# The projection stage's planner: reciprocal deviations gated on GpSimd, low parts kept off VectorE, and two turns of tokens in one slot

## The chip, the core and the metric

The kernel runs on one core of a Trainium2 chip. The metric is the device time of one execution in microseconds; lower is better. Engines are named as the profile names them: PE is TensorE (PEld is its weight load, which overlaps PE), DVE is VectorE, ACT is ScalarE, POOL is GpSimd, SP is SyncE. Every engine works through its own queue in the order in which the program wrote it, and waits where an operand is not there yet.

## What is computed

One transformer block on 2048 tokens of 640 features, in float32: a normalisation, attention with 32 heads of 20 features, a residual sum, a second normalisation, and a gated feed-forward part with 1728 inner features.

```python
def _layernorm(x, axis=-1, eps=1e-5):
    m = jnp.mean(x, axis=axis, keepdims=True)
    v = jnp.var(x, axis=axis, keepdims=True)
    return (x - m) / jnp.sqrt(v + eps)

qkv = x @ wqkv                       # x normalised: 2048x640 @ 640x1920
scores = jnp.einsum("bhqd,bhkd->bhqk", q, k) * (Dh ** -0.5)
o = jnp.einsum("bhqk,bhkd->bhqd", softmax(scores), v)
h = x + o @ wo
h2 = h + (silu(z @ w_gate) * (z @ w_up)) @ w_down    # z: h normalised
```

## The kernel before, in words

The tokens go in four chunks of 512, and each chunk in four tiles of 128. The kernel has three stages: the **projections** (q, k and v of all chunks), attention, and the feed-forward part. The change touches the projections alone, which fill roughly the first 324 us.

**Products in float32 precision.** Each operand is split into a high part (ScalarE, L97) and a low part, which is the operand less its high part (L98, on the engine that `split` is given). A product is three matmuls: high by high, high by low, low by high. `query_key` makes a block of 128 columns of q or k for a chunk (15 matmuls of 512 columns), `value` a tile of v (15 matmuls of 320 columns). All these are L573 in the profile. The array is used as two halves of 64 rows, and each of the 15 matmuls comes twice, once for each half, so that a block is 30 rows of the trace.

**The work list.** `work` is a list of 72 slots: blocks of chunk 0, then for each chunk its 10 blocks mixed with the 8 value tiles of the chunk before, then the last value tiles. Chunk c's first block stands in slot `begins(c) + 2` (slots 12, 30 and 48). In slots `begins(c) - 3` to `begins(c) + 1` the chunk's normalised tokens are turned (transposed), feature tile by feature tile, five in all, one to a slot.

**A turn** (`flip`, L787) is 16 small transposes on PE (L793) into two PSUM banks, two copies to SBUF and the high part on ScalarE (L801 twice, then L97 into `z_hi`), and the low part `z_lo` on VectorE or GpSimd (L98). `before_flip` asks the planner for two free banks first. Blocks and value tiles of the chunk need `z_hi` of all five turns at once, as their first five matmuls, and `z_lo` in their last five.

**Normalisation of a chunk** (`norm`, L759) is a list of 14 items, `lns`, handed out two to a slot: four of statistics (L133, L134 on VectorE), six that hold the eleven steps of the reciprocal deviation on 128x4 elements (`rstd_steps`: a first guess by integer arithmetic and three Newton steps, L107 on VectorE), and four that apply it (L765, on GpSimd for chunks 2 and 3). Turns start when `lns` is empty.

**Filling products.** Attention needs, for each query, the largest score ahead of the exponentials. Part of these score products is made in this stage, between the projection's matmuls, from finished blocks that were stored to DRAM and loaded again ("staged", `load_items`). GpSimd forms the difference of two staged key tiles in place (L433). Each pair of products is one or two matmuls (L195, L218), a rectification on ScalarE (L206, L232) and a sum with maximum on VectorE (L208 and L225, each with a short read of the maximum). VectorE's instruction frees the PSUM bank. There are eight banks; projections, turns and filling products share them.

**The planner.** `Halves` (L534) writes all this as one order. It keeps its own clock of each half of PE and of VectorE, ScalarE, GpSimd, SyncE and the DMAs, in `free`, with a fixed duration for each operation (for instance 1.3 us for a low part on GpSimd and 0.75 us on VectorE, L532), and issues whatever its clocks say is ready. So a change of one rule alters the order of PE, ScalarE, VectorE and GpSimd from there to the stage's end, though not what is computed. Which engine makes a low part is chosen in `second_part` (L661). It is called by `flip` for `z_lo` and by `keep` (L843), which stores a finished block: PSUM to SBUF (L352), high part (L97) and low part (L98) into a buffer that the trace calls `e`, `q_stk` or `v_stk`, whichever lent place is used.

Of the kernel before, what the change touches and what calls it, by code (L numbers as in the profile page):

```python
# [50 lines left out]
def tile_block(ctx: ExitStack, tc: tile.TileContext, x, wqkv, wo, wg, wu, wd, out):  # L51
# [287 lines left out]
    with tc.tile_pool(name="pa", bufs=2) as pa:  # L339
# [186 lines left out]
        def next_pair():  # L526
# [2 lines left out]
            queues = (others, early) if first else (early, others)  # L529
            return next((queue for queue in queues if queue and queue[0][0]()), None)  # L530

        SECOND = (("pool", 1.3), ("vector", 0.75))  # L532

        class Halves:  # L534
# [125 lines left out]

            def second_part(self, after):  # L661
                ends = [max(self.free[e], after, self.now()) + us for e, us in SECOND]
                if ends[1] + 1.0 < ends[0] and self.free["vector"] < after + 0.5:
                    return nc.vector, self.use("vector", SECOND[1][1], after)
                return nc.gpsimd, self.use("pool", SECOND[0][1], after)

# [92 lines left out]
        def norm(c):  # L759

            mv = pa.tile([P, TPC, 2], F32, name="mv")
            r, steps = rstd_steps(pa, mv[:, :, 1], TPC, "a")

            def apply(t):
                (nc.gpsimd if c > 1 else nc.vector).tensor_scalar(  # L765
                    xs[c * TPC + t], xs[c * TPC + t], mv[:, t, 0:1], r[:, t : t + 1],
                    op0=ALU.subtract, op1=ALU.mult,
                )

            return (  # L770
                [
                    (("vector", 1.1), lambda t=t: stats(pa, xs[c * TPC + t], mv[:, t, :]), c)
                    for t in range(TPC)
                ]
                + [(("vector", 0.35), lambda f=f, g=g: (f(), g()), c) for f, g in zip(steps[::2], steps[1::2] + [lambda: None])]
                + [
                    (("pool", 2.55) if c > 1 else ("vector", 0.75), lambda t=t: apply(t), c)
                    for t in range(TPC)
                ]
            )  # L780
# [161 lines left out]
        for at, (kind, c, *which) in enumerate(work):  # L942
# [70 lines left out]
                load_values(0, 0, NT - TPC)  # L1013
            last = any(at == begins(n) + 1 for n in range(1, NC))
            for _ in range(99 if last else 4 if 4 <= at < 7 else 2):
                if at >= 2 and lns and (pe.now() >= x_at[lns[0][2]] or last):
                    normed = pe.use(*lns[0][0], normed) + 0.2
                    lns.pop(0)[1]()
            for _ in range(99 if last else 1):
                if flips and not lns and (pe.now() >= normed or last):  # L1020
                    flip(*flips.pop(0))
            if at == len(work) - 6:
# [1078 lines left out]
```

## Time and profile before

| | us |
|---|---|
| median of 3 runs | 2024.7 |
| the 3 runs | 2026.38, 2024.70, 2023.99 |
| the profiled execution's own time | 2026.52 |
| its span, first to last instruction | 2024.7 |
| PE busy, of that span | 2002.5 |
| VectorE busy | 1620.2 |
| ScalarE busy | 1460.2 |
| GpSimd busy | 779.8 |
| granted PE clock (1 is full speed) | 1.00 |

All stretches of the trace are given from the span's start. A row of the timeline has the start, the duration (of all merged instructions), the engine, line and operation, what is written and read, the shapes, a count, and in brackets the idle time of the engine before it with what ended that. A row of the waits has who waited for whom, the total, how often, and the longest. A row of the groups has the count, then the busy time and the mean duration of one in ns, then idle time before. A PE matmul's end is modelled, so the start of the next weight load (PEld) shows a stop of PE better than the busy time does.

### The profile page before, as it was taken

What the parts mean: (1) busy time and instruction counts of PE and PEld (TensorE: products, weight loads), DVE (VectorE), ACT (ScalarE), POOL (GpSimd) and SP (SyncE); (2) the same over time, 40 slices, a digit from 0 to 9 for tenths busy, and PEclk for the clock granted to TensorE, in tenths of its full rate; (3) what the DMA queues carried; (4) which work ended last, traced back from release to release, by engine and by line L of the source; (5) the groups of instructions that cost most, each with busy time, mean ns of one, the idle gap of its engine ahead of it and who ended that gap; (6) DMA issues with size and microseconds to landing.
All of it is one profiled execution on the core that took longest, in us unless ns stands there. A gap on an engine that the chain in (4) does not pass through costs nothing.

```text
span 2024.7 us, 39120 instructions
## 1 busy us (share of the span) xinstructions
PE 2002.5 (99%) x13714; PEld 1237.8 (61%) x13714; DVE 1620.2 (80%) x3257; ACT 1460.2 (72%) x2944; POOL 779.8 (39%) x1075
## 2 busy tenths in 40 slices
PE   8999999999999999999999999999999999999998
PEld 7898896333333333333333333345598888888888
DVE  8869678888888888888888888886378666676667
ACT  4888888999999999999999999986633222212221
POOL 4454451243524334344520011011146444764555
PEclk9999999999999999999999999999999999999999
DMA  7866663433443534435333122221159654974542
GB/s 234 257 198 192 190 191 108 135 116 117 140 128 106 161 117 142 145 123 166 123 134 102 33 71 73 81 62 49 46 185 323 206 189 154 352 272 159 204 148 93
DMA packets 205205, 304.91 MB, mean 151 GB/s; under 512 B 47648, under 2 KB 82720, under 8 KB 203984
## 3 DMA queue, kind: packets, MB, share of 16 engines
q1 hardware_dynamic: 204768, 302.24, 45.7%
q8 instruction: 109, 1.79, 0.4%
q14 instruction: 88, 0.72, 0.1%
q10 hardware_dynamic: 240, 0.17, 0.0%
HBM read 205.78 MB, written 95.68 MB: 149 GB/s over the span
## 4 chain that ended last, share of the span: by engine, by line
PE 95%; DVE 2%; ACT 1%; issue 1%; POOL 1%; DMA 0%; SPq 0%; ACTq 0%; DVEq 0%; POOLq 0%
PE banks L1394 25%; PE banks L1384 17%; PE banks L1562 17%; PE banks L239 12%; PE banks L573 9%; PE banks L1656 8%; PE banks L1113 3%; PE banks L218 3%; PE banks L195 1%; PE banks L836 0%; PE banks L264 0%; DVE st L133 0%; DMA o_t<-o_d 0%; PE banks L1145 0%; PE banks L793 0%
## 5 line engine op out<-in xcount | busy, mean ns | idle before, releaser
L1390 ACT ACTIVATE probs<-banks 128x512 f32<-128x512 f32 x2048 | 1056.2, 612 | 58.1 <-PE banks L1384 25.9
L245 DVE TENSOR_REDUCE mx<-banks 128x1 f32<-128x512 f32 x1472 | 925.1, 684 | 116.3 <-PE banks L239 62.6
L1384 PE MATMUL banks<-q_stk,k_stk 62*128 62x512 f32 x2048 | 581.3, 429 | 1.1 <-ACT probs L1390 1.1
L1394 PE MATMUL banks<-probs,v_stk 128*32 128x512 f32 x4096 | 544.3, 604 | 0.0
L239 PE MATMUL banks<-k_stk,q_stk 60*128 60x512 f32 x1472 | 486.5, 438 | 0.2
L1384 PEld LDWEIGHTS banks<-q_stk,k_stk 62*128 62x128 f32 x2048 | 290.4, 185 | 284.4 <-ACT probs L1390 270.3
L239 PEld LDWEIGHTS banks<-k_stk,q_stk 60*128 60x128 f32 x1472 | 244.2, 184 | 162.5 <-DVE mx L245 127.1
L1780 DVE TENSOR_TENSOR tmp<-banks,tmp 128x512 f32<-128x512 f32 x208 | 141.1, 689 | 114.5 <-PE banks L1562 89.0
L1394 PEld LDWEIGHTS banks<-probs,v_stk 128*32 128x32 f32 x4096 | 80.9, 108 | 182.0 <-issue 170.1
L1656 PE MATMUL banks<-halves,yp 128*128 128x320 f32 x1032 | 178.7, 308 | 0.2 <-DVE h L1661 0.2
L1656 PEld LDWEIGHTS banks<-halves,yp 128*128 128x128 f32 x1032 | 165.1, 188 | 16.0 <-DVE h L1661 0.5
L1562 PE MATMUL banks<-t,units 128*128 128x512 f32 x624 | 162.7, 396 | 0.1
L98 POOL TENSOR_TENSOR yp<-y,yp 128x256 fp32r<-128x256 f32 x96 | 60.5, 630 | 190.4 <-ACT yp L97 176.2
L1562 PE MATMUL banks<-z,units 128*128 128x512 f32 x516 | 133.7, 394 | 0.0
L256 POOL CAST both<-neg 128x16 fp32r<-128x16 f32 x32 | 6.6, 208 | 312.0 <-PE banks L239 187.1
L1562 PEld LDWEIGHTS banks<-t,units 128*128 128x128 f32 x624 | 112.5, 188 | 18.9 <-DVE tmp L1780 0.4
L1661 DVE TENSOR_TENSOR h<-banks,h 128x320 f32<-128x320 f32 x248 | 109.9, 480 | 8.6 <-POOL h L1694 4.3
L225 DVE CUSTOM_DVE_ANT_0 q_stk<-banks,q_stk 128x512 f32<-128x512 f32 x140 | 92.5, 687 | 24.1 <-PE banks L218 14.5
L573 PE MATMUL banks<-z_hi,w_hi 64*128 64x512 f32 x380 | 105.6, 396 | 2.3 <-ACT z_hi L97 2.0
L573 PE MATMUL banks<-z_lo,w_hi 64*128 64x512 f32 x380 | 105.2, 393 | 0.0
L1562 PEld LDWEIGHTS banks<-z,units 128*128 128x128 f32 x516 | 93.2, 187 | 15.9
L573 PE MATMUL banks<-z_hi,w_lo 64*128 64x512 f32 x380 | 101.8, 391 | 0.0
(218 smaller groups left out, 2900.8 us busy)
## 6 DMA issues: line engine op xcount, KB each, us to landing
units<-w_d SPq DMA_DIRECT2D x186, 256.0 KB
w_d<-stage SPq DMA_DIRECT2D x106, 256.0 KB
halves<-j_d SPq DMA_DIRECT2D x70, 320.0 KB
k_stk<-qk_d SPq DMA_DIRECT2D x112, 160.0 KB
j_d<-stage SPq DMA_DIRECT2D x42, 320.0 KB
q_stk<-qk_d SPq DMA_DIRECT2D x64, 160.0 KB
k_stk<-qk_d SPq DMA_DIRECT2D x112, 80.0 KB
rb<-r_d SPq DMA_DIRECT2D x32, 256.0 KB
```

What stands on the lines that cost most here:

```text
L218: nc.tensor.matmul(ps, q[rows, pair, t * P : (t + 1) * P], k[rows, pair, :], start=True, stop=True)
L225: nc.vector.tensor_tensor_reduce(out=place, in0=ps, in1=place, scale=1.0, scalar=LEAST, op0=ALU.add, op1=ALU.max, accum_out=mx[:, b, pair, ...
L239: nc.tensor.matmul(ps, queries[u][rows, pair, t * P : (t + 1) * P], keys[u // NC][rows, pair, kc * CH : (kc + 1) * CH], start=True, stop=True,
L245: nc.vector.tensor_reduce(mxs[u][:, b, pair, t, kc : kc + 1], ps, axis=AX.X, op=ALU.max)
L573: product = nc.tensor.matmul(job["ps"][:, :out], lhs, rhs, start=(half == 0 and i == 0), stop=(half == 1 and i == job["n"] - 1),)
L1384: nc.tensor.matmul(ps, keys[u // NC][rows, p, kt * P : (kt + 1) * P], queries[u][rows, p, :], start=True, stop=True,)
L1390: nc.scalar.activation(probs[p][:, b, :], ps, AF.Exp, scale=scale)
L1394: nc.tensor.matmul(acc[32 * j : 32 * j + 32, :], values[u // NC][:, kt, j * VW : j * VW + 32], probs[j // 2][:, j % 2, :], start=(kt == 0) ...
L1562: nc.tensor.matmul(ps.rearrange("p (t n) -> p t n", t=TPC), w[k][:, i], z[k][:, :, j], start=(first and m == 0), stop=(last and m == len(n ...
L1656: nc.tensor.matmul(ps, a, b, start=(n == 0), stop=(n == len(pairs) - 1))
L1661: nc.vector.tensor_tensor(out=h, in0=ps, in1=h, op=ALU.add)
L1780: add = lambda out, ps, x: nc.vector.tensor_tensor(out=out, in0=ps, in1=x, op=ALU.add)
```

## The change

Three rules of the planner are altered.

```diff
+        NEWTON = "vector", 0.35
         SECOND = (("pool", 1.3), ("vector", 0.75))
...
             def second_part(self, after):
                 ends = [max(self.free[e], after, self.now()) + us for e, us in SECOND]
+                ends[1] = max(ends[1], self.free["pool"] + SECOND[1][1])
                 if ends[1] + 1.0 < ends[0] and self.free["vector"] < after + 0.5:
                     return nc.vector, self.use("vector", SECOND[1][1], after)
                 return nc.gpsimd, self.use("pool", SECOND[0][1], after)
...
-                + [(("vector", 0.35), lambda f=f, g=g: (f(), g()), c) for f, g in zip(steps[::2], steps[1::2] + [lambda: None])]
+                + [(NEWTON, lambda f=f, g=g: (f(), g()), c) for f, g in zip(steps[::2], steps[1::2] + [lambda: None])]
...
             for _ in range(99 if last else 4 if 4 <= at < 7 else 2):
-                if at >= 2 and lns and (pe.now() >= x_at[lns[0][2]] or last):
+                alone = not lns or lns[0][0] != NEWTON or pe.free["pool"] <= pe.now()
+                if at >= 2 and lns and (pe.now() >= x_at[lns[0][2]] and alone or last):
                     normed = pe.use(*lns[0][0], normed) + 0.2
                     lns.pop(0)[1]()
-            for _ in range(99 if last else 1):
+            for _ in range(99 if last else 1 + any(at == begins(n) for n in range(1, NC))):
                 if flips and not lns and (pe.now() >= normed or last):
                     flip(*flips.pop(0))
```

- An item of the reciprocal deviation is handed out only in a slot at which the planner's clock of GpSimd has run out, or in the slot `begins(c) + 1`, in which everything left is handed out.
- VectorE's end of a low part is reckoned from GpSimd's clock too. Since VectorE is taken only when its end is more than 1.0 us ahead of GpSimd's, and the two ends now differ by 1.3 - 0.75 = 0.55 us at most, VectorE is not taken at all: the seven low parts that it had in this stage after slot 8 are all GpSimd's.
- In slot `begins(c)` two turns may be made instead of one.

Counted over the whole program, PE, ScalarE and SyncE keep their numbers of instructions; VectorE has seven fewer, and GpSimd seven more.

On VectorE, in chunk 2's turns (the end of `begins(2) - 2` and of `begins(2) - 1`), the difference of the two orders reads as follows. L225 is the sum with maximum of a filling product, which frees a bank, and its second row the read of the maximum.

```order
 L225 ISA v_stk_117,mx_126<-banks,v_stk_117 128x512
 L225 ISA mx_126 128x1
-L98 TENSOR_TENSOR z_lo<-xt,z_hi 128x512
 L225 ISA q_stk,mx_126<-banks,q_stk 128x512
 L225 ISA mx_126 128x1
 L225 ISA q_stk,mx_126<-banks,q_stk 128x512
 L225 ISA mx_126 128x1
-L98 TENSOR_TENSOR v_stk_117<-v_stk_117 128x512
 L225 ISA v_stk_117,mx_126<-banks,v_stk_117 128x512
 L225 ISA mx_126 128x1
```

Both low parts have left VectorE's queue; nothing stands in their place.

On PE, the last turn of chunk 2 and what follows it. In the order of before, `z_hi_583` belongs to chunk 1 and `z_hi_1790` to chunk 2; 512 columns are a block, 320 a value tile.

```order
L573 MATMUL banks_100<-z_lo_584,w_hi_163 128x512
L573 MATMUL banks_100<-w_hi_163,z_hi_583 128x320
L793 MATMUL banks_100<-ident_101,xt_895 128x64 x8
L218 MATMUL banks_100<-k_stk0_116,raw_672 128x512
L573 MATMUL banks_100<-w_hi_163,z_hi_583 128x320
L573 MATMUL banks_100<-z_hi_1790,w_hi_163 128x512
L573 MATMUL banks_100<-w_hi_163,z_hi_583 128x320 x2
L573 MATMUL banks_100<-z_hi_1790,w_hi_163 128x512
```

In the order of the change, lines are one to three higher, and the chunks' parts are `z_hi_583` and `z_hi_1776`.

```order
L574 MATMUL banks_100<-z_hi_583,w_hi_163 128x512 x2
L795 MATMUL banks_100<-ident_101,xt_884 128x64 x8
L574 MATMUL banks_100<-z_hi_583,w_hi_163 128x512
L795 MATMUL banks_100<-ident_101,xt_884 128x64 x8
L574 MATMUL banks_100<-w_hi_163,z_hi_583 128x320 x2
L574 MATMUL banks_100<-z_hi_583,w_lo_164 128x512
L574 MATMUL banks_100<-w_hi_163,z_hi_583 128x320 x2
L574 MATMUL banks_100<-z_hi_583,w_lo_164 128x512
L218 MATMUL banks_100<-raw_674,raw_672 128x512
```

Two turns now follow each other, one slot earlier; the first matmul that reads `z_hi_1776` stands 26 rows (32 matmuls) after the last transposes, where before it was the third row after them.

On PE, the last turns of chunk 3 in the order of the change. Here the reciprocal deviations of the chunk come later, so that the turns begin two slots later (at `begins(3) - 1`), and the last two are in the last slot; `z_hi_2907` is chunk 3's.

```order
L574 MATMUL banks_100<-z_lo_1777,w_hi_163 128x512
L795 MATMUL banks_100<-ident_101,xt_2047 128x64 x8
L574 MATMUL banks_100<-w_hi_163,z_hi_1776 128x320 x2
L795 MATMUL banks_100<-ident_101,xt_2047 128x64 x8
L574 MATMUL banks_100<-z_hi_2907,w_hi_163 128x512
L574 MATMUL banks_100<-w_hi_163,z_hi_1776 128x320
L574 MATMUL banks_100<-z_hi_2907,w_hi_163 128x512
L574 MATMUL banks_100<-w_hi_163,z_hi_1776 128x320 x2
```

Before, one turn stood there instead of two, and it too was followed at once by the chunk's first block.

## Prediction, made before the run

> **What bounds the kernel now.** I read the page's chain first, then the busy times by stretch. The chain of the whole execution is PE:
>
> ```profile
> ## 4 chain that ended last, share of the span: by engine, by line
> PE 95%; DVE 2%; ACT 1%; issue 1%; POOL 1%; DMA 0%; SPq 0%; ACTq 0%; DVEq 0%; POOLq 0%
> ```
>
> The reader is to see that nothing but a shorter PE order, or fewer stops of PE, can shorten the kernel. The columns below are PE, PEld, DVE, ACT and POOL busy. The first row is the projection stage, the next two are stretches of it, the last is attention:
>
> ```profile
> 20.00:324.00 304.00, 298.10 (x2811) 276.32 (x2810) 238.33 (x833) 241.36 (x530) 139.94 (x117) 1.00 0.67 207
> 120.00:150.00 30.00, 27.90 (x276) 25.88 (x274) 19.75 (x55) 25.96 (x53) 14.40 (x11) 1.00 0.62 193
> 150.00:180.00 30.00, 28.46 (x276) 26.45 (x275) 28.68 (x87) 22.94 (x42) 13.63 (x9) 1.00 0.66 211
> 340.00:360.00 20.00, 20.00 (x144) 7.71 (x136) 17.93 (x30) 19.46 (x40) 0.42 (x2) 1.00 0.01 2
> ```
>
> Attention has PE busy in all its 20 us, so it hides nothing that the stage ahead of it loses: a microsecond saved in the projections starts attention a microsecond earlier, and I carry it to the end of the kernel in full. In the projections PE stops for little, the clock is 1.00, and GpSimd is idle for over half of the time. So the next view is who PE's weight loads wait for in that stage:
>
> ```profile
> PEld banks L218 <- DVE mx L225: 3.0, 6, 2.0
> PEld banks L573 <- ACT z_hi L97: 2.6, 2, 1.4
> PEld banks L793 <- DVE mx L208: 1.9, 4, 1.2
> PEld banks L573 <- DVE mx L225: 1.3, 1, 1.3
> PEld banks L195 <- DVE mx L208: 0.4, 1, 0.4
> PEld banks L264 <- POOL e L98: 0.4, 1, 0.4
> ```
>
> That is 6.6 us for VectorE (3.0 + 1.9 + 1.3 + 0.4) and 2.6 us for the high part of a turn, most of it in five single waits. They are what the change can win. GpSimd itself is waited for once, 0.4 us.
>
> **Part 1: low parts leave VectorE.** What each of them costs now:
>
> ```profile
> L98 DVE TENSOR_TENSOR v_stk<-v_stk 128x512 fp32r<-128x512 f32 x2 | 3.6, 1794 | 0.0
> L98 DVE TENSOR_TENSOR e<-e 128x512 fp32r<-128x512 f32 x3 | 3.3, 1094 | 6.0 <-ACT e L97 6.0
> L98 DVE TENSOR_TENSOR z_lo<-xt,z_hi 128x512 fp32r<-128x512 f32 x1 | 1.2, 1160 | 1.4 <-ACT z_hi L97 1.4
> L98 DVE TENSOR_TENSOR q_stk<-q_stk 128x512 fp32r<-128x512 f32 x1 | 0.7, 691 | 0.6 <-ACT q_stk L97 0.6
> L98 POOL TENSOR_TENSOR e<-e 128x512 fp32r<-128x512 f32 x15 | 19.5, 1297 | 53.3 <-ACT e L97 45.1 <-DMA xt<-qk_d 5.0 <-DMA raw<-qk_d 3.2
> ```
>
> Seven instructions, 3.6 + 3.3 + 1.2 + 0.7 = 8.8 us of VectorE, though alone one takes 0.69 us. On GpSimd the seven take 7 x 1.30 = 9.1 us of the 164 us (304 - 139.94) in which it is idle. Two of the big waits of PE stand right behind such an instruction. VectorE, GpSimd and PE at 52 us and at 130 us:
>
> ```profile
> 51.94 1.78 DVE L98 TENSOR_TENSOR v_stk<-v_stk 128x512 fp32r<-128x512 f32 x1
> 51.43 1.75 POOL L433 TENSOR_TENSOR k_stk<-k_stk 128x512 fp32r<-128x512 f32 x1
> 54.11 0.13 PEld L793 LDWEIGHTS banks<-ident,xt 64*128 64x128 f32 x1 [1.17 <-DVE mx L208]
> ...
> 127.55 1.16 DVE L98 TENSOR_TENSOR z_lo<-xt,z_hi 128x512 fp32r<-128x512 f32 x1 [1.43 <-ACT z_hi L97]
> 129.85 1.81 DVE L98 TENSOR_TENSOR v_stk<-v_stk 128x512 fp32r<-128x512 f32 x1
> 125.60 5.51 POOL L433 TENSOR_TENSOR k_stk<-k_stk,raw 128x512 fp32r<-128x512 f32 x4
> 132.32 0.18 PEld L573 LDWEIGHTS banks<-w_hi,z_hi 64*128 64x128 f32 x1 [1.33 <-DVE mx L225]
> ```
>
> VectorE's 0.69 us instruction takes 1.8 us while GpSimd works, the sums with maximum behind it free their banks late, and PE stops for 1.17 and 1.33 us. With those instructions gone from VectorE's queue the sums start at once. I count both waits as won: **-2.5 us**, between 0 (if the next sum is late for another reason; ScalarE, which feeds it, is busy 25.96 of 30 us there) and -6.6 (all waits for VectorE go). What is late next: the stored blocks. On GpSimd they take 0.6 us longer and queue. Nothing of PE reads them directly; they go by a DMA to filling products some slots later. I cost that at nothing, with the filling products that are ready meanwhile as cover.
>
> **Part 2: reciprocal deviations.** The third big wait is theirs, in chunk 3:
>
> ```profile
> 159.40 1.24 DVE L107 TENSOR_SCALAR v_a<-mv 128x4 f32<-128x4 f32 x1
> 160.67 1.22 DVE L107 TENSOR_SCALAR r_a<-v_a 128x4 int32<-128x4 int32 x1
> 161.93 1.19 DVE L107 SCALAR_TENSOR_TENSOR t_a<-r_a,v_a 128x4 f32<-128x4 f32 x1
> 163.15 0.16 DVE L107 TENSOR_TENSOR t_a<-t_a,r_a 128x4 f32<-128x4 f32 x1
> 159.31 2.56 POOL L433 TENSOR_TENSOR raw<-raw,k_stk 128x512 fp32r<-128x512 f32 x2 [4.34 <-DMA raw<-qk_d]
> 161.82 1.28 POOL L98 TENSOR_TENSOR v_stk<-v_stk 128x512 fp32r<-128x512 f32 x1
> 163.97 0.18 PEld L218 LDWEIGHTS banks<-raw,q_stk 60*128 60x128 f32 x1 [1.96 <-DVE mx L225]
> ```
>
> Three GpSimd instructions of 1.28 us, and three steps that end with them and take 1.2 us where the fourth takes 0.16: 3.65 instead of about 0.5 us, in the stretch where VectorE is busy 28.68 of 30 us. PE stops for 1.96 us. But the new rule is no guard against this very case. It asks the planner's clock of GpSimd, and the instruction that was in the way had waited 4.34 us for a DMA: the trace's GpSimd runs later than a fixed duration says. What helps is that the steps now stand elsewhere, 14 sums later, and only in slots for which the planner has nothing left on GpSimd. The other stretched step is in chunk 2:
>
> ```profile
> 83.08 0.79 DVE L107 TENSOR_SCALAR v_a<-mv 128x4 f32<-128x4 f32 x1
> ```
>
> It takes 0.6 us over the 0.16 of an undisturbed one and PE did not stop behind it. I take the 1.96 us as won and put one such stretch of 0.6 us back on the path: **-1.4 us**, between -1.96 (no step is met) and +1.2 (three are met again, all on the path: 3 x 1.05 = 3.2 less 1.96).
>
> On this the Trainium skill speaks against the gate as it is built. SBUF — State Buffer, "Who interferes with whom", says that a VectorE instruction with two SBUF inputs, or one in a two-port mode, and a GpSimd instruction that reads SBUF exclude each other, and that whichever issues first holds up the other. The rows above agree (0.16 us against 1.2). By that rule only what GpSimd really does when a step issues counts, so the gate is worth its 1.96 us only if the real idle time meets the planner's; by the planner's own view it would be worth 1.96 in full, and my -1.4 lies between.
>
> **Part 3: two turns in one slot.** The last turn of chunks 2 and 3 makes PE wait for its high part. ScalarE and PE, first at 140 us, then PE at 225 us:
>
> ```profile
> 139.34 0.61 ACT L352 ACTIVATE e<-banks 128x512 f32<-128x512 f32 x1
> 139.98 0.63 ACT L97 ACTIVATE e<-e 128x512 fp32r<-128x512 f32 x1
> 140.51 0.64 ACT L801 ACTIVATE xt<-banks 128x256 f32<-128x256 f32 x2
> 141.19 0.63 ACT L97 ACTIVATE z_hi<-xt 128x512 fp32r<-128x512 f32 x1
> 141.87 0.18 PEld L573 LDWEIGHTS banks<-z_hi,w_hi 64*128 64x128 f32 x1 [1.18 <-ACT z_hi L97]
> ...
> 225.47 0.18 PEld L573 LDWEIGHTS banks<-z_hi,w_hi 64*128 64x128 f32 x1 [1.40 <-ACT z_hi L97]
> ```
>
> A finished block (0.64 + 0.53 us, from start to start) and the turn (0.68 + 0.63) stand in line on ScalarE. In chunk 2 the change puts 32 matmuls between the last turn and the first use. By the stretch from 120 to 150 us (276 matmuls in 30 us, 0.109 us each) they take 3.5 us against 2.6 us for two turns on ScalarE (2 x 1.31): covered, **-1.2 us**. In chunk 3 the last two turns are both in the last slot, and the block follows at once. ScalarE has one more turn to do there, 1.3 us, but PE has it to make too and no sum of a filling product comes between, so I let that wait stand: 0, between -1.4 and +1.3. Chunk 1 has no such wait to win.
>
> **The order as a whole.** From chunk 1's third turn on all four orders differ, with the same number of matmuls, so PE streams as long as before. New waits of banks are to be expected where old ones were; no row can show them. The nearest rows are the five waits themselves, 1.17 to 1.96 us. I put back one of 1.4 us, between 0 and 5.6 (all four that I counted as won return: 1.17 + 1.33 + 1.96 + 1.18).
>
> **Sum.** -2.5 - 1.4 - 1.2 + 1.4 = -3.7 us. The profiled execution took 2026.5 us with a span of 2024.7, so it would take 2022.8 with a span of 2021.0. It lies 1.8 us over the median of the runs, 2024.7; the forecast for the median is 2024.7 - 3.7 = 2021.0.
>
> **Rivals.**
>
> *The waits move, and nothing is won.* VectorE is busy 28.68 of 30 us from 150 to 180; a queue that full makes PE wait somewhere whichever instruction is taken out. For it: ScalarE is at 25.96 of 30 where two of the waits stand. Against it: the waits are few and single, each behind one long instruction. All four return, and the time is 2024.7, give or take 1.5.
>
> *VectorE's relief reaches further.* All 6.6 us of waits for VectorE go, and chunk 2's 1.2: -7.8, 2016.9. For it: VectorE loses 8.8 us of low parts and up to 3.8 us of stretched steps. Against it: 1.0 us of these 6.6 are many waits of some 0.2 to 0.4 us, which look like the rhythm of the order.
>
> *GpSimd becomes the engine that is waited for.* The seven parts stand ahead of staged differences (L433) and of `z_lo` in its one queue. It decides from the point where its lateness, 9.1 us more of work and its waits for DMAs, exceeds what the planner leaves between a part and its use on PE:
>
> ```profile
> POOL k_stk L433 <- DMA k_stk<-qk_d: 15.1, 3, 8.2
> ```
>
> A part queued behind the longest of these is 8.2 us late. At most PE sees all 9.1 us: 9.1 - 3.7 = +5.4, 2030.1. Against it: GpSimd is idle for 54% of the stage, and PE now waits for it 0.4 us in all. A page of the Trainium skill stands on this side: GPSIMD Engine Reference, "4.1 Engine selection", puts elementwise work on VectorE and calls GpSimd about twice as slow for two inputs. The trace agrees on the ratio (1.297 against 0.691 us); by that rule alone the seven parts would cost 7 x 0.6 = 4.2 us.
>
> *The gate does nothing of what it says*: it is part of the first rival, as the steps would be met by GpSimd as before and only other waits go.
>
> **How the numbers follow.** Forecast, 0.55, with a range of its own from -6 to -1.5 (2018.7 to 2023.2). Waits move, 0.22. Relief reaches further, 0.15. GpSimd is waited for, 0.08. A measurement of this kernel can tell about 0.2%, 4.05 us, from no change, so faster means under 2020.65. Somewhat under half of the forecast's chance lies there (0.25), and all of the second rival's (0.15): 0.40. Slower by over 0.2%: 0.08. The rest, 0.52, is within 0.2%. The range goes from the second rival's 2016.9, less 0.9 for the scatter of the runs, 2016.0, to the first's upper end and as much scatter, 2027.0; GpSimd's case is left out.
>
> **What would show it.** Part 1: no L98 on VectorE's timeline from 50 to 324 us but those that read a bank, and no PEld wait over 1 us for L208 or L225 during the turns of chunks 1 and 2. Part 2: L107's largest durations under 0.8 us, at most one over 1. Part 3: the wait of L573 for `z_hi` once instead of twice, in chunk 3. The stage should end (last L573) 3 to 4 us earlier, and attention take as long as before. I am wrong if waits for POOL appear on PE, if a new wait over 1.5 us stands at another place, or if the stage ends earlier and the kernel does not.

## The result, and the profile after

| | before | after |
|---|---|---|
| median of 20 runs each | 2028.45 us | 2022.93 us |
| lowest and highest | 2023.99 to 2033.09 | 2019.93 to 2027.77 |
| ratio, 95% interval | | 0.9977 (0.9971 to 0.9983) |
| the profiled execution's own time | 2026.52 | 2023.31 |
| its span | 2024.7 | 2021.5 |
| last projection product starts at | 323.81 | 320.31 |
| from there to the end | 1700.92 | 1701.18 |

The kernel became 0.23% faster: 4.7 us by the ratio, 5.5 us by the medians, 3.2 us by the two profiled spans. In these two profiled executions the whole difference lies in the projections, whose end came 3.5 us earlier; the rest took as long as before. The windows of the changed kernel (columns as before) show the same three stretches:

```profile
20.00:324.00 304.00, 301.25 (x2822) 281.35 (x2825) 228.27 (x829) 243.58 (x538) 150.37 (x125) 0.99 0.67 209
120.00:150.00 30.00, 30.00 (x302) 28.96 (x299) 22.70 (x72) 27.94 (x57) 16.65 (x14) 1.00 0.71 216
150.00:180.00 30.00, 30.00 (x291) 28.16 (x289) 27.40 (x96) 26.56 (x51) 8.94 (x7) 1.00 0.66 205
340.00:360.00 20.00, 20.00 (x145) 7.90 (x146) 17.95 (x30) 19.58 (x40) 0.42 (x2) 1.00 0.01 2
```

By the modelled ends, PE has no stop left from 120 to 180 us. VectorE has 10 us less to do in the stage and GpSimd 10 us more. One figure of the first row is new: the granted clock is 0.99, not 1.00. The waits of PE's weight loads in the stage:

```profile
PEld banks L574 <- ACT z_hi L97: 2.1, 2, 1.4
PEld banks L218 <- ACT q_stk L232: 0.9, 4, 0.3
PEld banks L195 <- DVE mx L208: 0.7, 1, 0.7
PEld banks L795 <- DVE xt L767: 0.5, 1, 0.5
PEld banks L218 <- DVE mx L225: 0.4, 2, 0.2
```

Waits for VectorE fell from 6.6 us to 1.7 (these three rows and a smaller one of 0.2), and none is over 0.7. PE does not wait for GpSimd. Summed over all releasers (idle times of the weight loads over 0.15 us, from 20 us to the last projection product), the waits are 6.05 us, against 12.13 before. So 6.1 us of waits went, but the stage won only 3.5. The difference lies at the first row, chunk 3's `z_hi`. ScalarE's row of turns there, and the two weight loads that wait for it:

```profile
211.51 0.60 ACT L352 ACTIVATE e<-banks 128x512 f32<-128x512 f32 x1
212.14 0.63 ACT L97 ACTIVATE e<-e 128x512 fp32r<-128x512 f32 x1
212.68 0.64 ACT L803 ACTIVATE xt<-banks 128x256 f32<-128x256 f32 x2
213.35 0.63 ACT L97 ACTIVATE z_hi<-xt 128x512 fp32r<-128x512 f32 x1
213.89 0.64 ACT L803 ACTIVATE xt<-banks 128x256 f32<-128x256 f32 x2
214.56 0.63 ACT L97 ACTIVATE z_hi<-xt 128x512 fp32r<-128x512 f32 x1
...
214.03 0.28 PEld L574 LDWEIGHTS banks<-z_hi,w_hi 64*128 64x128 f32 x1 [1.43 <-ACT z_hi L97]
215.24 0.28 PEld L574 LDWEIGHTS banks<-z_hi,w_hi 64*128 64x128 f32 x1 [0.71 <-ACT z_hi L97]
```

Two turns stand back to back on ScalarE behind a finished block, 1.21 us each, and PE has to stop for each of them. What happened to the clock right then (windows, the granted clock is the third figure from the end):

```profile
210.65:214.07 3.42, 2.25 (x29) 1.67 (x25) 0.00 (x0) 3.36 (x8) 2.89 (x3) 1.00 0.71 190
214.07:217.48 3.41, 3.10 (x16) 2.70 (x18) 0.45 (x1) 1.57 (x4) 2.51 (x3) 0.50 1.00 333
217.48:220.90 3.42, 3.42 (x22) 3.38 (x21) 0.89 (x5) 1.63 (x3) 2.52 (x2) 0.50 0.12 44
```

For 6.83 us PE ran at half its clock. That costs (6.83 - 0.71) / 2 = 3.1 us, an estimate, since 0.71 us of it were the second wait. Waits less 6.1, clock plus 3.1, makes -3.0; the stage ended 3.5 us earlier. The kernel before had no such fall anywhere in its projections.

### The profile page after: what moved, and what is told of

Its sections match the earlier page's. It is cut to its first block, busy times and chain, and to the rows that moved or that the text cites. A ratio compares the mean times of both kernels' runs of the same rounds, so it can differ in the third digit from the quotient of the medians.

```text
span 2021.5 us, 39114 instructions
## 1 busy us (share of the span) xinstructions
PE 2003.8 (99%) x13714; PEld 1241.6 (61%) x13714; DVE 1613.0 (80%) x3250; ACT 1458.9 (72%) x2944; POOL 785.4 (39%) x1082
## 4 chain that ended last, share of the span: by engine, by line
PE 94%; DVE 2%; DMA 1%; ACT 1%; POOL 1%; issue 1%; ACTq 0%; SPq 0%; POOLq 0%; DVEq 0%
PE banks L1397 25%; PE banks L1387 17%; PE banks L1565 16%; PE banks L239 12%; PE banks L574 9%; PE banks L1659 8%; PE banks L1116 3%; PE banks L218 3%; PE banks L195 1%; DMA xt<-in_A_x 0%; PE banks L838 0%; DMA z_d<-halves 0%; PE banks L264 0%; DVE st L133 0%; PE banks L795 0%
## 5 line engine op out<-in xcount | busy, mean ns | idle before, releaser
L1393 ACT ACTIVATE probs<-banks 128x512 f32<-128x512 f32 x2048 | 1056.2, 612 | 58.5 <-PE banks L1387 23.5
L98 POOL TENSOR_TENSOR yp<-y,yp 128x256 fp32r<-128x256 f32 x96 | 60.3, 628 | 190.7 <-ACT yp L97 176.5
L225 DVE CUSTOM_DVE_ANT_0 q_stk<-banks,q_stk 128x512 f32<-128x512 f32 x138 | 90.6, 687 | 32.4 <-PE banks L218 20.9
```

Source lines behind the costliest of these rows:

```text
L225: nc.vector.tensor_tensor_reduce(out=place, in0=ps, in1=place, scale=1.0, scalar=LEAST, op0=ALU.add, op1=ALU.max, accum_out=mx[:, b, pair, ...
L1393: nc.scalar.activation(probs[p][:, b, :], ps, AF.Exp, scale=scale)
```

## The experiments

Each was timed in five rounds beside the kernel before; ratios are to the runs of before on the same chip. "End" is the start of the last projection product, "waits" the sum as above, both from the one profiled execution.

| | low parts | gate | two turns | ratio (95%) | end, us | waits, us |
|---|---|---|---|---|---|---|
| before | | | | 1 | 323.8 | 12.1 |
| after | x | x | x | 0.9977 (0.9971 to 0.9983) | 320.3 | 6.1 |
| `again` (the same) | x | x | x | 0.9966 (0.9948 to 0.9983) | 319.5 | 6.8 |
| `only_parts` | x | | | 0.9993 (0.9985 to 1.0002) | 322.0 | 9.4 |
| `parts_blind` | x, order of before | | | 0.9994 (0.9982 to 1.0007) | 321.6 | 10.9 |
| `only_gate` | | x | | 0.9987 (0.9978 to 0.9996) | 319.4 | 8.1 |
| `only_turns` | | | x | 1.0028 (1.0017 to 1.0040) | 309.3, then 18.6 | 6.6 |
| `one_turn` | x | x | | 0.9979 (0.9971 to 0.9988) | 319.7 | 6.5 |
| `vector_parts` | | x | x | 0.9979 (0.9968 to 0.9990) | 320.8 | 10.8 |
| `no_gate` | x | | x | 0.9959 (0.9943 to 0.9975) | 318.1 | 6.1 |
| `gate_c2` | x | chunks 1, 2 | x | 0.9955 (0.9942 to 0.9968) | 314.5 | 4.9 |
| `turns_all` | x | x | more room | 0.9965 (0.9952 to 0.9978) | 317.5 | 7.4 |
| `fill` | x | x | x | 0.9976 (0.9967 to 0.9986) | 322.2 | 6.3 |
| `late` | x | | x | 0.9961 (0.9947 to 0.9974) | 316.2 | 5.4 |

The column of ends needs care. The same weight load, the 59th of the program, starts anywhere from 21.5 us (`vector_parts`) to 23.5 us (`fill`), so ends of single executions compare to about 1 us. All kernels but `only_turns` make the same products before the end (`fill` eight more). Counted from that load, their ends range over 9.2 us, from 292.2 to 301.5 us. Less PE's waits, less half of the stretches at 0.5 outside the waits, and in `fill` less its added matmuls, 287.6 to 290.4 us are left. So waits and clock together, an estimate from these traces, account for the ends to within some 1.5 us. What follows the stage scatters as well: six of these thirteen traces show 3.41 us at half clock at about 1445 us, three also one right behind the stage. A ratio over a few executions therefore need not follow the ends.

My theory after the first look: the gain is VectorE's queue and chunk 2's turn, as predicted, but the gate delays chunk 3's turns by two slots, leaves two of them to the last slot, and loses there a good part of what it won. Rivals: the gate itself brings the gain, or any new order scatters the waits by chance.

### Is it the gate that crowds chunk 3's turns?

`no_gate`:

```diff
-                alone = not lns or lns[0][0] != NEWTON or pe.free["pool"] <= pe.now()
+                alone = True
```

> The changed kernel without the gate: the steps of the reciprocal deviation are handed out as before, while the low parts stay on GpSimd and two turns may share a slot. Chunk 3's turns then start two slots earlier and none is left for the last slot. Theory (the gate's worth is eaten by what it delays): PE's two waits for chunk 3's z_hi (1.43 and 0.71 us at 212 to 215 us in the changed kernel) go, the granted clock does not fall to 0.5 behind them (6.83 us at half speed, worth 3.4 us), but steps of L107 are stretched by GpSimd again (total after 40 us near 7 us instead of 4.25). The stage should end 2 to 5 us before the changed kernel's 320.3 us, and the kernel take about 2 to 5 us less. Rival (the gate brings the gain): stretched steps put a wait of about 2 us on PE again, the stage ends at 321 to 323 us, and the kernel takes 1 to 3 us more than the changed one.

Both waits for `z_hi` were gone and the end came 2.3 us earlier than in the changed kernel, with the stretched steps back: 7.72 us of L107 after 40 us, against 4.25. PE stopped for only 0.72 us behind those of chunk 3, and for 1.00 us behind those of chunk 2. The gate was no gain here: without it the kernel is at 0.9959, though this interval overlaps the changed kernel's.

`gate_c2` leaves the gate off for chunk 3 alone:

```diff
-                alone = not lns or lns[0][0] != NEWTON or pe.free["pool"] <= pe.now()
+                alone = not lns or lns[0][0] != NEWTON or lns[0][2] == 3 or pe.free["pool"] <= pe.now()
```

> The changed kernel with the gate on chunks 1 and 2 alone; chunk 3's steps are handed out as before, so that its turns lie two slots earlier and none in the last. Theory (the gate costs its gain only where it crowds chunk 3's turns): no wait for z_hi of over 0.4 us at 210 to 217 us, so 1.5 to 2.1 us less of PE's waits than in the changed kernel, and where the clock keeps 1.0 the stage ends at 315.5 to 318 us; steps of chunk 3 may be stretched again by up to 1.5 us in all, which PE does not wait for or waits for once by under 1 us. Kernel 1 to 3.5 us under the changed one. Rival (the gate is worth nothing anywhere, and without it altogether the kernel is as good): as the kernel without the gate, within 1 us of its median. Second rival: chunk 3's steps, stretched, put 1.5 to 2 us back on PE, and the kernel is no better than the changed one.

The end came at 314.5 us, earlier than that of any kernel with the same products before it, and the median was 2019.54 us (5 executions) against 2023.78 of `again` (7) in the same session. Its interval lies wholly below the changed kernel's 0.9971, but overlaps that of `again`. No clock fell in this trace before the end. VectorE's steps of chunk 3 and what PE had to wait behind them:

```profile
152.86 1.23 DVE L107 TENSOR_SCALAR r_a<-v_a 128x4 int32<-128x4 int32 x1
154.12 1.21 DVE L107 SCALAR_TENSOR_TENSOR t_a<-r_a,v_a 128x4 f32<-128x4 f32 x1
...
156.24 0.18 PEld L218 LDWEIGHTS banks<-raw,q_stk 60*128 60x128 f32 x1 [0.67 <-DVE mx L225]
156.85 0.18 PEld L218 LDWEIGHTS banks<-raw,q_stk 60*128 60x128 f32 x1 [0.32 <-DVE mx L225]
```

Two steps were stretched, where it had been three before, and cost PE 1.0 us in two stops instead of 1.96 in one. So what a stretched step costs depends on whether the sum behind it holds a bank that PE is about to need. That the end also came earlier than `no_gate`'s is not shown to be the gate's doing on chunk 2: two of that chunk's steps were stretched here too (1.09 and 1.19 us), and what is missing is a wait behind chunk 2's statistics, which `fill` shows below.

`turns_all` keeps the gate and lets the slots ahead of the last take up to two and three turns:

```diff
-            for _ in range(99 if last else 1 + any(at == begins(n) for n in range(1, NC))):
+            for _ in range(99 if last else 1 + any(at == begins(n) - 1 for n in range(1, NC)) + 2 * any(at == begins(n) for n in range(1, NC))):
```

> The changed kernel with room for more turns in the two slots before the last (up to two, then up to three), so that chunk 3 has none left for the last slot though the gate delays it. Theory: z_hi of chunk 3 is ready before it is used, PE's waits of 1.43 and 0.71 us there go, the clock keeps 1.0, and the stage ends 3 to 5.5 us earlier than the changed kernel's 320.3 us. Rival (the fall of the clock is not tied to that wait): the clock falls at about 214 us all the same, and at most 2.1 us are won. Second rival (three turns in a slot make a jam on ScalarE): a wait of PE for ScalarE or VectorE of over 2 us stands at the turns, and nothing is won.

No wait for `z_hi` anywhere, clock 1.00, end 2.8 us earlier, a little under what was expected. PE waits 1.35 us for VectorE at 186 us: behind two steps of chunk 3 that were stretched to 0.92 and 1.22 us although the gate was in. Three kernels that take chunk 3's turns out of the last slot, two by leaving out its gate and one by more room for turns, all end 2.3 to 5.8 us earlier (3.4 to 5.9 counted from the common load): in these traces the loss lies at the last slot.

### Does the fall of the clock belong to that stop?

`again` is the changed kernel, executed once more.

> The changed kernel itself, executed and profiled again beside the others on one chip. Theory A (the fall of the clock at 214 us belongs to that execution: PE's two stops for z_hi recur in every execution, but a fall behind them does not): the waits of about 1.4 and 0.7 us for z_hi stand at 212 to 215 us again, and the clock keeps 1.0 there or falls, one as likely as the other; without the fall the stage ends at 316.5 to 318 us instead of 320.3. Theory B (the stop always makes the clock fall): 0.5 for 3.4 to 6.8 us from about 214 us again, the stage ends at 319.5 to 321 us. The wait of VectorE's statistics for chunk 2's tokens at 75 us, 0.70 us on PE before, is expected anywhere from 0 to 2.4 us, since it hangs on a DMA.

PE's weight loads, and the windows of 3.41 us:

```profile
214.28 0.18 PEld L574 LDWEIGHTS banks<-z_hi,w_hi 64*128 64x128 f32 x1 [1.42 <-ACT z_hi L97]
215.49 0.18 PEld L574 LDWEIGHTS banks<-z_hi,w_hi 64*128 64x128 f32 x1 [0.91 <-ACT z_hi L97]
```

```profile
213.25:216.66 3.41, 1.72 (x15) 1.47 (x17) 0.06 (x1) 2.61 (x7) 3.41 (x3) 1.00 0.85 263
216.66:220.07 3.41, 3.41 (x24) 3.41 (x22) 1.25 (x4) 1.63 (x3) 2.15 (x3) 0.50 0.71 231
220.07:223.49 3.42, 3.42 (x32) 2.95 (x32) 2.92 (x9) 2.22 (x5) 0.58 (x1) 1.00 0.23 92
```

The same two waits, and the clock fell again behind them, now 2.6 us later and for 3.41 us. So it was no accident of one execution, and it is not fixed to the stop's moment either. Of 27 executions of the changed kernel two show a mean granted clock of 1.000; of 70 executions of the kernel before, timed beside the experiments, 19 do. The two have spans of 2018.4 and 2018.6 us, the 19 a mean of 2024.7: 6.2 us apart, about what the waits alone lost. Two executions are few for this.

`fill` adds work: behind the last turns of chunk 3, eight matmuls of 512 columns into a bank that nobody reads.

```diff
+            if at == begins(3) + 1:
+                scratch = banks[:, pe.take()]
+                for _ in range(8):
+                    nc.tensor.matmul(scratch, ones_r, w_hi[:, 0, :CH], start=True, stop=True)
```

> The changed kernel with work added: eight matmuls of 512 columns into a bank that nobody reads, on PE behind the last two turns of chunk 3, where PE waited for z_hi. They take about as long as the wait (1.4 to 2 us) and need nothing that is late. Theory (a stop of PE of over 1.4 us in a few us is what makes the clock fall there): PE does not stop for more than 0.6 us between 211 and 216 us, the clock does not fall to 0.5 there in the profiled execution, and the chunk's first block starts no later; the stage ends 2 to 4 us before the changed kernel's 320.3 us although PE has more to do, and over the runs the mean clock is nearer to 1.0 than the changed kernel's (1 of 20 runs at 1.000). Rival (the fall is not tied to the stop): the clock falls as often as before, and the stage ends within 0.7 us of 320.3 us, or later by what was added.

PE waited for `z_hi` no more and the clock stayed at 1.00 from 207 to 222 us. But the end came late, 322.2 us, against expectation, since the clock fell at another place, on a stop that I had taken for a small one. VectorE, PE's weight load, and the windows there:

```profile
76.23 0.89 DVE L133 BATCH_NORM_STATS2 st<-xt 128x6 f32<-128x320 f32 x2 [3.32 <-DMA xt<-in_A_x]
...
78.71 0.18 PEld L195 LDWEIGHTS banks<-raw 60*128 60x128 f32 x1 [2.36 <-DVE mx L208]
```

```profile
75.44:78.85 3.41, 1.41 (x14) 1.05 (x12) 2.55 (x9) 0.39 (x1) 0.48 (x1) 1.00 0.97 372
78.85:82.26 3.41, 3.41 (x20) 3.22 (x22) 3.34 (x15) 2.16 (x5) 0.58 (x1) 0.50 0.76 241
```

Chunk 2's statistics stand in VectorE's queue before their tokens have landed, and the sums behind them hold PE's banks. In the changed kernel this wait is the 0.70 us for L208; it was 0.84 in `again`, 1.15 in `no_gate` and 2.36 here: the new wait that I had put back without knowing its place. With 2.1 us of added matmuls the kernel was no faster than the changed one. So in this one trace no stop meant no fall at 214 us, as in the two of the changed kernel a stop meant a fall; that filling the stop pays is not shown.

`late` is `no_gate` with these statistics one slot later:

```diff
-                if at >= 2 and lns and (pe.now() >= x_at[lns[0][2]] and alone or last):
+                if at >= (14 if lns and lns[0][2] == 2 else 2) and lns and (pe.now() >= x_at[lns[0][2]] and alone or last):
```

> The kernel without the gate (low parts on GpSimd, two turns in a slot) with one thing more: chunk 2's statistics are handed out from slot 14 on instead of 13, behind more of VectorE's sums. Theory (the statistics wait in VectorE's queue for the DMA of the chunk's tokens, 1.7 to 3.3 us, and the sums behind them keep PE's banks for 0.7 to 2.4 us): no idle time of VectorE for the tokens over 0.5 us between 70 and 80 us, no wait of PE for L208 of over 0.5 us there; the stage ends 0.7 to 2 us before the 318.0 us of the kernel without the gate, and the kernel takes 0.5 to 2 us less than its 2020. Rival (the tokens come later still, or the turns of chunk 2 get crowded): a wait of over 1 us for the tokens or for chunk 2's z_hi, and no gain.

```profile
75.99 0.88 DVE L133 BATCH_NORM_STATS2 st<-xt 128x6 f32<-128x320 f32 x2
```

No bracket: VectorE did not wait for the tokens, PE's waits for L208 were 0.2 us in all, and the end came 1.9 us before `no_gate`'s. The mechanism is as expected, but over the runs `late` and `no_gate` cannot be told apart (0.9961 and 0.9959).

### What is each part worth alone?

`only_parts` is the kernel before with the rule on low parts:

```diff
+                ends[1] = max(ends[1], self.free["pool"] + SECOND[1][1])
```

> The kernel before with the rule on low parts alone; the turns keep their slots, and chunk 3 keeps one in the last slot. Theory (the stretched low parts made PE's waits of 1.17 and 1.33 us): no L98 of VectorE from an SBUF buffer, those two waits go and nothing takes their place, the stage ends 1.5 to 4 us before the 323.8 us of before, and the kernel takes 1.5 to 4 us less. PE's waits for z_hi (1.18 us in chunk 2, 1.40 us in chunk 3) stay. Rival (the order alone moves waits): the total of PE's waits for VectorE stays at 5 us or more, at other places, and the kernel is within 1.5 us of before.

Both waits went, the end came 1.8 us earlier, the two for `z_hi` stayed (1.55 and 1.39 us). The wait of 1.96 us went as well, without any gate: one step of chunk 3 was stretched (1.22 us) instead of three. Over the runs 0.07%, which the interval does not separate from nothing.

`parts_blind` keeps before's order and moves the seven low parts only:

```diff
                 if ends[1] + 1.0 < ends[0] and self.free["vector"] < after + 0.5:
-                    return nc.vector, self.use("vector", SECOND[1][1], after)
+                    return nc.gpsimd, self.use("vector", SECOND[1][1], after)
```

> The order of before, instruction for instruction on PE and ScalarE; only the seven low parts that VectorE had are made by GpSimd, and the planner does not know of it, so nothing else is moved. This tells the relief itself from the new order. Theory: PE's waits of 1.17 us at 54 us and 1.33 us at 132 us fall under 0.4 us each, the others (1.18, 1.96, 1.40) stay within 0.3 us; the stage ends 1.8 to 3 us before 323.8 us, the kernel takes about 2.5 us less. Rival (GpSimd, which now has two low parts in line where the planner counts one, is late): PE waits for POOL, or for a filling product whose staged blocks come late, by 1 us or more, and no more than 1 us is won. Second rival: the two waits stay over 0.8 us, since ScalarE is what makes the sums late.

PE's weight loads at the two places and at a new one:

```profile
54.37 0.18 PEld L195 LDWEIGHTS banks<-k_stk 60*128 60x128 f32 x1 [0.48 <-DVE mx L208]
...
72.14 0.18 PEld L195 LDWEIGHTS banks<-raw 60*128 60x128 f32 x1 [1.01 <-POOL raw L433]
```

The wait of 1.17 us became 0.48, that of 1.33 us was gone, and the one of 1.96 us, which was expected to stay, fell to 0.50 as well: two steps of chunk 3 met GpSimd (1.22 and 0.75 us) instead of three. The end came 2.2 us earlier. The rival's price is there too: 1.0 us for GpSimd, in a place where the planner did not know what it had to do, and 1.1 us for ScalarE at 314 us. Over the runs 0.06%, again not to be told from nothing.

`vector_parts` is the changed kernel without that line:

```diff
-                ends[1] = max(ends[1], self.free["pool"] + SECOND[1][1])
```

> The changed kernel without the rule on low parts: VectorE makes seven of them again, gate and two turns stay. Theory (a low part on VectorE is stretched to 1.1 to 1.8 us by GpSimd, and PE waits for the sums behind it): one to three waits of PE for VectorE of 1.0 to 1.7 us return, each behind an L98 of VectorE; total of PE's waits for VectorE 2.5 us over the changed kernel's. Chunk 3's turns lie in slots that leave one for the last, but not two. If the fall of the clock hangs on PE's wait for z_hi there, it may be spared: then the two cancel and the stage ends within 1.5 us of 320.3 us; if it falls as well, the stage ends 2 to 3 us later. Rival (low parts on VectorE cost nothing; the two waits were of the order alone): no wait behind an L98, and the stage ends no later than 319 us where the clock keeps 1.0.

VectorE, GpSimd and PE at three of the places that matter:

```profile
51.31 1.77 DVE L98 TENSOR_TENSOR v_stk<-v_stk 128x512 fp32r<-128x512 f32 x1
53.48 0.14 PEld L794 LDWEIGHTS banks<-ident,xt 64*128 64x128 f32 x1 [1.19 <-DVE mx L208]
...
155.38 1.16 DVE L107 TENSOR_SCALAR r_a<-v_a 128x4 int32<-128x4 int32 x1
156.58 1.20 DVE L107 SCALAR_TENSOR_TENSOR t_a<-r_a,v_a 128x4 f32<-128x4 f32 x1
155.19 2.57 POOL L433 TENSOR_TENSOR raw<-raw,k_stk 128x512 fp32r<-128x512 f32 x2 [1.45 <-DMA raw<-qk_d]
158.63 0.18 PEld L218 LDWEIGHTS banks<-raw,q_stk 60*128 60x128 f32 x1 [1.48 <-DVE mx L225]
...
214.08 1.63 DVE L98 TENSOR_TENSOR z_lo<-xt,z_hi 128x512 fp32r<-128x512 f32 x1 [3.00 <-ACT z_hi L97]
216.38 0.18 PEld L218 LDWEIGHTS banks<-k_stk 60*128 60x128 f32 x1 [1.06 <-DVE mx L225]
```

Four waits of over 1 us. Two stand behind a stretched low part (1.19 and 1.06 us), as expected. The other two, 1.32 us at 84 us and 1.48 us at 159 us, stand behind two stretched steps each, although the gate was in. Waits for VectorE are 8.2 us, more than before. No long wait for `z_hi` in chunk 3 and no fall of the clock; so the end is within 0.5 us of the changed kernel's, and the two cancel, as expected.

`only_gate` is before with the gate (and the two lines that name `NEWTON`):

```diff
-                if at >= 2 and lns and (pe.now() >= x_at[lns[0][2]] or last):
+                alone = not lns or lns[0][0] != NEWTON or pe.free["pool"] <= pe.now()
+                if at >= 2 and lns and (pe.now() >= x_at[lns[0][2]] and alone or last):
```

> The kernel before with the gate alone: reciprocal deviations in slots for which GpSimd's clock has run out, low parts and single turns as before. Theory (the gate is worth its stretched steps where it does not crowd the turns): total of L107 after 40 us 4 to 5.5 us instead of 7.36, the wait of 1.96 us behind the steps at 164 us goes; the turns of chunk 3 keep their slots, so no second turn in the last slot; the low parts on VectorE (ten of them now) still make 1 to 3 waits of over 1 us. Stage end 0.5 to 2.5 us before the 323.8 us of before. Rival (the gate is worth nothing, the rest of the change brings it all): stage end within 0.5 us of before or later.

The steps were all undisturbed (3.59 us of L107 after 40 us), the wait of 1.96 us went, the wait behind the low part at 54 us was still 1.15. But the gate had moved chunk 2's turns by one slot, and PE waited there for `z_hi`:

```profile
138.91 0.18 PEld L574 LDWEIGHTS banks<-z_hi,w_hi 64*128 64x128 f32 x1 [2.17 <-ACT z_hi L97]
```

`one_turn` is the changed kernel with one turn to a slot:

```diff
-            for _ in range(99 if last else 1 + any(at == begins(n) for n in range(1, NC))):
+            for _ in range(99 if last else 1):
```

> The changed kernel with one turn per slot, as before. Theory (two turns win chunk 2's wait of 1.18 us and nothing else): the wait for chunk 2's z_hi of 1.0 to 1.4 us returns near 142 us; chunk 3's last two turns are in the last slot still, with the wait for z_hi and, if that wait makes the clock fall, the fall at about 214 us. The stage ends 0.8 to 1.6 us later than the changed kernel's 320.3 us, the kernel takes about 1.2 us more. Rival (a changed order moves PE's waits at random): the total of PE's waits is anywhere between 6 and 12 us, and the end of the stage with it, with no tie to chunk 2.

```profile
137.89 0.18 PEld L574 LDWEIGHTS banks<-z_hi,w_hi 64*128 64x128 f32 x1 [0.99 <-ACT z_hi L97]
139.10 0.18 PEld L574 LDWEIGHTS banks<-z_hi,w_hi 64*128 64x128 f32 x1 [0.62 <-ACT z_hi L97]
```

Chunk 2's wait was back, 1.61 us in all, at the place where the change had covered it. Chunk 3's two waits were 0.24 and 0.91 us in this trace, and no clock fell behind them, so, against expectation, the end is not later than the changed kernel's; over the runs the two are equal.

`only_turns` is before with that line's other form:

```diff
-            for _ in range(99 if last else 1):
+            for _ in range(99 if last else 1 + any(at == begins(n) for n in range(1, NC))):
```

> The kernel before with two turns in one slot alone; VectorE keeps low parts (five of them) and the steps are handed out as before. Theory: both waits for z_hi go, 1.18 us in chunk 2 and 1.40 us in chunk 3, since here no turn of chunk 3 is left for the last slot; the waits behind VectorE's low parts and stretched steps stay (one to three of 1 us or more). The stage ends 1.5 to 3.5 us before the 323.8 us of before, the kernel takes 1.5 to 3.5 us less. Rival (new waits take their place): waits of PE in total 11 us or more, and the kernel within 1 us of before.

This was wrong. Both waits for `z_hi` went, and the one of 1.96 us with them, and the last projection product came at 309.3 us, but behind it stood 18.6 us of filling products that the planner had not found place for earlier. The windows there:

```profile
310.00:320.00 10.00, 9.42 (x31) 4.59 (x29) 9.22 (x29) 8.61 (x16) 0.00 (x0) 0.70 0.47 162
320.00:328.00 8.00, 8.00 (x24) 5.16 (x24) 7.67 (x33) 7.16 (x19) 0.00 (x0) 0.50 0.00 0
```

With no projection products between them, PE makes 3 of them in a microsecond, the clock falls to 0.5 for 20.5 us, and the first score product of attention starts at 327.84 us instead of 323.38. Why the planner was left with them I did not trace. Alone, this part is a loss of 0.28%; beside the rule on low parts it belongs to the fastest kernels. The parts do not add: 0.07% + 0.13% - 0.28% is a loss, and together they won 0.23%.

## Why the prediction came out as it did

- **Part 1, -2.5 us: right for the waits.** Both went in the changed kernel, and with the order of before 2.0 of their 2.5 us did (`parts_blind`). `vector_parts` brought the first of them back behind the same stretched L98. What this part is worth over the runs is not shown: alone it gave 0.07% and 0.06%, within the noise.
- **Part 2, -1.4 us: the wait went, but the gate is not shown to have removed it.** One stretched step was left, as put back, and PE did not stop behind it. (In `again`, the same kernel, it was 1.27 us, and PE stopped for 0.46 us.) VectorE's step and GpSimd's instruction beside it:

```profile
87.11 0.83 DVE L107 SCALAR_TENSOR_TENSOR r_a<-t_a,r_a 128x4 f32<-128x4 f32 x1
...
86.62 1.29 POOL L433 TENSOR_TENSOR k_stk<-k_stk 128x512 fp32r<-128x512 f32 x1 [4.03 <-DMA k_stk<-qk_d]
```

  The step ends within 0.03 us of GpSimd's instruction, which a DMA had made 4 us late: the planner's clock could not know, as the prediction said. The wait of 1.96 us also went in kernels that have no gate (`only_parts`, `only_turns`). With the gate, several steps were stretched all the same in `vector_parts` and `turns_all`, and PE stopped for 1.48 and 1.35 us behind those of chunk 3. Beside the other two parts but without the gate, PE lost 0.7 to 1.0 us there (`no_gate`, `gate_c2`). So the gate is not the guard that it was meant to be, and I had missed its price: it delays the steps, then the turns.
- **Part 3, chunk 2, -1.2 us: right for the wait**, which came back in `one_turn`; the time over the runs did not. **Chunk 3, 0: the wait's size was in its bounds, its consequence was not.** The wait grew from 1.40 to 2.14 us (+0.7). What failed is the term that closed it, "so I let that wait stand: 0, between -1.4 and +1.3": with the clock that fell behind the longer stop, another 3.1 us, it was +3.8 in the profiled execution.
- **The order as a whole, +1.4: too much**, by the profiled execution. One new wait of over 0.5 us came, 0.70 us, at 76 us; in `again` it was 0.84.
- **Sum, -3.7.** The waits fell by 6.1 us, 2.4 more than the sum, and the clock, which had no term, took 3.1. The forecast of the end's move (3 to 4 us; it was 3.5) was met by two errors that cancel, which is luck. The forecast median of 2021.0 us rests on three early runs of the kernel before; its median over 20 is 2028.45, 3.75 us higher, so that 2022.93 lies near it by luck too. The move itself was 4.7 to 5.5 us instead of 3.7.
- **The rivals.** GpSimd was not waited for. "The waits move" does not hold for the changed kernel, whose waits are halved; in `vector_parts`, with almost as many microseconds of waits as before, they did move. "Relief reaches further" was the better forecast for VectorE's waits (6.6 to 1.7). The prediction argued against it with 1.0 us of small waits; its own rows leave 6.6 - 1.17 - 1.33 - 1.96 = 2.1 us. A kernel with another order and none of the three rules was not run, so how much of the 1.96 us and of the small waits any new order would have won stays open.

## What to carry to other kernels

When a rule delays a step, follow the delay to the next deadline behind it; here the gate delayed the steps, and the turns after them came too late. Price a stop of PE with the clock that it may cost, and look for that in the granted clock by stretch before explaining why a sum of waits and a span disagree. A guard that asks a planner's clock guards only as well as that clock follows the chip. Parts of a planner's change are worth only what they are worth together, so take one out as well as put one in: the change without its gate on chunk 3 was ahead of the whole in the same session.

## What the runs showed of the hardware

In the projections the granted clock of PE fell to 0.5 after stops of 2.1 to 2.4 us in all, and stayed there for one or two stretches of 3.41 us; in `only_turns` it stayed there for six. The work in such a stretch can be counted from the traces: the columns that PE streamed between two possible changes of the clock, in matmuls of 512 columns on half of the array. In the projections of the 14 traces, apart from the first stretch after the start, a usual stretch has some 28. The three falls (`after`, `again`, `fill`) follow stretches with 10.8, 10.6 and 8.7; among the over 1200 others the lowest have 11.4 (`only_gate`) and 12.6 (`vector_parts`). Over the whole program there are 13 falls, behind stretches with 8.7 to 12.5, and three of 11.4, 11.9 and 12.2 without a fall. There the two groups overlap, and attention's products of 32 columns are counted like those on half of the array.

Whether a stop is followed by a fall seems therefore to hang on where it lies in such a stretch. Single stops of 2.17 us in `only_gate` and of 1.96 us in the kernel before reached over two stretches and drew nothing; 1.42 and 0.91 us in one stretch of `again` did. That it is the work in a stretch and not the length of a stop that decides is read from these counts (some records may be missing) and was not tried by itself.

The Trainium skill, TensorE: Matmul & The Clock Gate, "What's actually happening", gives the stretch: a window of 3413 ns that runs freely. The traces agree (falls of 3.41, 6.83 and 20.48 us). The same page of the Trainium skill, section "HAM oscillation — how this bites in real kernels", has the rule that no gap should exceed some 3.4 us; here stops that add up to 2.1 and 2.3 us were enough, and the measurement decides.
